# One bias table per distance, written as skewed DRAM rows, in a fused attention and token mixer

## The chip, the cores and the metric

The kernel runs on one core of one Trainium2 chip. The metric is the device time of one execution in microseconds (us). The kernel before has a median of 658.86 us over three runs (658.49 to 1035.87).

## The reference

Four batches of eight heads of attention over 576 positions with 64 columns a head, with a learned bias on the scores, and behind it a token mixer and a channel mixer over the 512 columns of a position:

```python
rel = (pos[:, None] - pos[None, :]).astype(np.float32)
psi_rel = np.log1p(np.abs(rel))
psi_i = np.log1p(np.maximum(pos[:, None].astype(np.float32), 1.0))
x = (psi_rel / psi_i)[..., None]
h = np.maximum(x @ w1 + b1, 0.0)          # 32 hidden values for each (i, j)
bias = h @ w2                             # 8 heads
scores = scores + bias.transpose(2, 0, 1)[None]
...                                       # softmax over j, times v
h = np.maximum(xt @ w_tok1, 0.0) @ w_tok2
u = x + h.transpose(0, 2, 1)
h2 = np.maximum(u @ w_ch1, 0.0) @ w_ch2
return u + h2
```

The bias depends on the query i and on the distance |i - j| alone, and is the same for all batches: 8 x 576 x 576 numbers. Since psi_i is positive, relu(w1 psi_rel / psi_i + b1) is relu(w1 psi_rel + b1 psi_i) / psi_i, and this is how the kernel computes it: rectify first, divide at the end.

## The kernel before

**The bias stage** (lines 457 to 488) works on 36 blocks of 16 queries. Partition p of a working tile holds one of 32 hidden units for one of four queries, so a block has four tiles of 128 x 576. `lw` holds w1 log1p(|distance|) over 1148 columns, each group of 32 partitions shifted by one column for its query; `rectify` (L440) cuts the window of 576 columns that belongs to the block and applies relu(window + b1 psi_i). Three of the four tiles are done on VectorE (DVE, L446), the fourth on ScalarE (ACT, L444), fixed. `mm` (L465, matmuls on L468) contracts the 32 hidden units with w2 into 8 heads: 8 fp32 matmuls of 288 columns, two halves for each of the four tiles, into the four quarters of one of two PSUM pairs, so that a pair holds 16 queries x 8 heads on its partitions. `over` (L471, on ACT at L474 or DVE at L476) multiplies by 8 / psi_i and writes one of 10 SBUF buffers (`eb`). `put` (L478) stores it to DRAM (`bd`) as 128 rows of 576 numbers, one contiguous 288 KB. 8 / psi_i itself is made by `inverse` (L451): a reciprocal and a product on DVE over 36 columns, a planned step that every `over` waits for.

Beside it, eight transfers of a padded copy of `v` (640 KB each) feed the 80 bf16 matmuls of L502, from whose diagonal a scale for `v` is taken.

**The attention** runs 16 units (two heads of one batch). Four times, for each pair of heads, `bias_load` (L644) reads the bias from DRAM: four transfers of 576 KB (128 queries x 2 heads, 4608 contiguous bytes a partition) and two small ones. For each 128 queries: scores (L717), bias and row maximum on DVE (L726), exp on ACT (L739), transposes on the tensor engine (L768) or, for two of five chunks, by DMA (L757), the products with `v` (L795 to L797). All bias matmuls come ahead of the first scores (`drawn`).

**The mixers**: the token mixer follows each unit; the channel mixer (L1017 to L1019, L1047 to L1049) has the last 300 us to itself.

**The order of the work** is not written by hand: each step is given costs per engine (`on`), a due time out of the table `DUE` (relative to a base of its block or unit), and what it follows, and `Plan.order` simulates the engines and emits the steps in the order found. A step with several engines (`over`) is given to the one that would end it first. Each engine, and SyncE and ACT as issuers of DMAs, then runs its instructions in that order, waiting where something is not there yet.

Of the kernel before, what the change touches and what calls it, by code (L numbers as in the profile page):

```python
# [8 lines left out]
F32 = mybir.dt.float32  # L9
# [14 lines left out]
TAB = 1148  # L24
# [11 lines left out]
SLACK = 0.129  # L36
STAY = 63.41
# [4 lines left out]
TURN = 1.5  # L42
# [11 lines left out]
ON = {'dlo': {'P': 1.9},  # L54
      'norm': {'V': (0.35, -36.79), 'A': (0.88, 3.18)},
      'over': {'A': 0.65, 'V': (0.72, 56.73)},
      'vh': {'P': (0.7, -16.17), 'V': (0.4, 23.01), 'A': (0.6, -13.17)},
      'vl': {'P': (1.36, 74.11)}}
DUE = {'blk': 46.13,
       'blkn': 2.08,  # L60
       'rect': -232.71,
       'bmm': -134.22,
       'over': -120.58,
       'put': -73.24,
       'bl': -42.04,
       'bln': 5.97,
       'sums': -151.84,
       'sumsn': 8.17,
       'measw': 90.24,
       'measwn': 4.78,  # L70
       'amax': 104.25,
       'scales': 323.07,
       'scalet': -281.84,
       'scalec': -178.66,
       'fill': -14.62,
       'fill1': 162.6,
       'tok': -57.19,
       'tokn': 3.24,
       'dec1': 79.36,
       'dec2': 61.91,  # L80
       'dec3': 106.38,
       'dec4': 116.76,
       'dec5': -136.21,
       'load_k': 105.83,
       'load_q': -18.77,
       'split_k': -79.64,
       'split_q': 4.13,
       'load_v': -169.03,
       'prep_v': 43.7,
       'prep_vh': -255.82,  # L90
       'prep_vl': 312.44,
       'scores': -150.45,
       'biased': 127.67,
       'exp': 18.59,
       'hi': -44.42,
       'lo': -62.4,
       'turn': -60.26,
       'flip': -86.15,
       'fliphi': -282.11,
       'flip2': 4.2,  # L100
       'fliplo': 90.47,
       'back': 106.94,
       'norm': -39.66,
       'mix0': -165.12,
       'mix1': 14.09,
       'relu': 5.56,
       'mix2': -169.29,
       'mix2b': -31.55,
       'store': 8.59,
       'w1': 54.35,  # L110
       'w1n': 17.85,
       'U0': 98.45,
       'U0n': -0.8,
       'U1n': -20.63,
       'U1': 4.3,
       'U2': 346.79,
       'Un': 3.06,
       'U3': 76.01,
       'U4': 222.06,
       'u1': 171.18,  # L120
       'u2': 58.41,
       'u3': 147.24,
       'u4': 38.89,
       'u5': 75.81,
       'G': 366.02,
       'G0': 89.88,
       'G0n': 7.58,
       'g1': 58.66,
       'g2': 70.33,
       'ur': 38.78,  # L130
       'w2m': -44.97,
       'w2mn': 7.09}
# [123 lines left out]
def attention_mixer(ctx, tc, qT, kT, v, cst, lg, ident, wt1, wt2, wc1, wc2, out, dump=None):  # L256
# [106 lines left out]
    with tc.manual_schedule():  # L363
# [45 lines left out]
        eb_t = [slots[:, 3 if i < 4 else 1, S * (i % 4 if i < 4 else i - 4):][:, 0:S] for i in range(EB_BUFS)]  # L409
        cs, lw, wf = (slots[:, 3, 4 * S + a:4 * S + b] for a, b in ((0, 190), (190, 190 + TAB), (190 + TAB, 222 + TAB)))  # L410
# [4 lines left out]
        bd = [ud.tile([128 if c < NCH else LEFT, NH * S], F32, name=f"bd{c}") for c in range(NCH + 1)]  # L415
# [35 lines left out]
        def inverse(e):  # L451
            V.reciprocal(out=ips, in_=ips)
            V.tensor_scalar(out=ips, in0=ips, scalar1=8.0, scalar2=None, op0=ALU.mult)

        ips_ok = add({"V": 0.4}, DUE["blk"] + DUE["over"], inverse)
        sums_all, mms = [], []
        for n, (c, o) in enumerate([(c, o) for c in range(NCH + 1) for o in range(8 if c < NCH else 4)]):
            q0 = 128 * c + 16 * o
            t = DUE["blk"] + DUE["blkn"] * n
            hs = Hold("rect")  # L460
            room = add({"-": 0.0}, t, lambda e: None, after=[room], take=[hs])
            rs = [add({"A": 0.68} if g == 3 else {"V": 0.47}, t + DUE["rect"], rectify(hs, g, q0 + 4 * g, 4 * n + g), after=[room], port=True) for g in range(4)]
# [18 lines left out]
            m = add({"T": 1.05}, t + DUE["bmm"], mm, after=rs, take=[ph], free=[hs], mode=3)  # L481
# [3 lines left out]
            bias_s.setdefault(c, []).append(add(wire("put", 1.0), t + DUE["put"], put, after=[v_], free=[eh]))  # L485
            bias_all.extend(bias_s[c][-1:])
            if n == 0:
                m2 = big.tile([128, 32], F32, name="m2")
                last, late = None, []
                vh_ = Hold("bank")  # L490
                for i in range(8):
                    h = Hold("sums")

                    def load(e, i=i, h=h):
                        ENG[e].dma_start(out=staging(h.i, 1280).rearrange("p (a x) -> p a x", a=2), in_=v[2 * i:2 * i + 2].rearrange("a p x -> p a x"))

                    def sums(e, i=i, h=h):

                        t = staging(h.i, 1280).bitcast(BF16).rearrange("p (n t) -> p n t", t=2)[:, :, 1]
                        for k in range(10):  # L500
                            x = t[:, k * 128:(k + 1) * 128]
                            PE.matmul(out=banks[vh_.i][:, 0:128], lhsT=x, rhs=x, start=(i == 0 and k == 0), stop=(i == 7 and k == 9))  # L502

                    x = add(wire("sums", 2.1), DUE["sums"] + DUE["sumsn"] * i, load, take=[h])
                    late.append((x, i))
                    last = add({"T": 0.68}, DUE["sums"] + DUE["sumsn"] * i + 6, sums, after=[x, last], take=[vh_] if i == 0 else [], free=[h], use=[vh_])
                    sums_all.append(last)
# [135 lines left out]

        def bias_load(hp, t0):  # L644
# [19 lines left out]
        def unit(u):  # L664
# [37 lines left out]
            for c in range(NCH + 1):  # L702
# [42 lines left out]
                if dma:  # L745
# [15 lines left out]
                    turned_s.append(add({"X": 1.8}, t + DUE["turn"], turn, after=[s], take=ta[:1], free=[p2]))  # L761
# [360 lines left out]
def lay_out(q, k, v, w1, b1, w2, moe_w_tok1, moe_w_tok2, moe_w_ch1, moe_w_ch2):  # L1122
    import numpy as np

    def heads(x):
# [17 lines left out]
    m = np.minimum(np.abs(np.arange(TAB)[None, :] - 572 - np.arange(4)[:, None]), S - 1)  # L1143
    lg = np.repeat(lrel[m], 32, axis=0)
# [6 lines left out]
        "qT": qq, "kT": kk, "v": vv,  # L1151
# [22 lines left out]
```

## Time and profile before

| | |
|---|---|
| median of the runs | 658.86 us |
| the profiled execution | 660.83 us |
| its span, first to last instruction | 659.0 us |
| PE (TensorE), busy | 624.8 us |
| DVE (VectorE), busy | 439.1 us |
| ACT (ScalarE), busy | 373.7 us |
| POOL (GpSimd), busy | 285.0 us |
| moved by DMA | 101.87 MB |
| mean granted TensorE clock | 0.984 of full |

The profiled execution is one run with the hardware profiler on; 1.8 us of it lie outside the span. Times in the rows below count from the start of the span. Busy time of the PE is from modelled ends of matmuls: a busy PE is not a PE at its peak.

### The profile page before, as it was taken

The page shows a single profiled execution, that of the slowest core. Times are in us where ns is not written, and L with a number is a line of the kernel's source. Part 1 is how long each engine was busy: PE and PEld are TensorE (multiplying, and loading weights), DVE is VectorE, ACT ScalarE, POOL GpSimd, SP SyncE. Part 2 cuts the span into 40 slices and gives each one's busy share as a digit, 9 for nine tenths or more (in the row PEclk, how much of TensorE's full clock was granted, in tenths as well). Part 3 has the DMA queues.
Part 4 walks back from the last instruction along what each step waited for, and adds up shares of the span by engine and source line. Part 5 has one row for each costly group of instructions (what it writes and reads, how often), then busy time and mean ns, then how long its engine had stood idle before and what let it go on. Part 6 is the DMA issues. An engine that isn't in the chain of part 4 may idle for free.

```text
span 659.0 us, 16970 instructions
## 1 busy us (share of the span) xinstructions
PE 624.8 (95%) x6820; PEld 421.6 (64%) x6820; DVE 439.1 (67%) x1125; ACT 373.7 (57%) x665; POOL 285.0 (43%) x328
## 2 busy tenths in 40 slices
PE   3988798799999999999999999999999999999996
PEld 1433587699898998988998864444444444465442
DVE  5799679988999899999999887877510220121000
ACT  5889668877887989888887644554311220021000
POOL 3020568795556878888743551665800000000000
PEclk9899789999999999999999999999999999999999
DMA  9997845699985945455544599656242001110211
GB/s 331 304 325 258 214 95 143 188 263 262 257 215 169 280 110 143 144 131 161 116 85 108 141 318 303 209 162 168 49 127 65 33 0 33 64 33 12 82 52 32
DMA packets 88511, 101.87 MB, mean 155 GB/s; under 512 B 49392, under 2 KB 58864, under 8 KB 88432
## 3 DMA queue, kind: packets, MB, share of 16 engines
q1 hardware_dynamic: 78784, 80.04, 43.7%
q10 hardware_dynamic: 9648, 20.75, 10.7%
q8 instruction: 53, 0.87, 0.6%
q14 instruction: 26, 0.21, 0.1%
HBM read 69.69 MB, written 20.05 MB: 136 GB/s over the span
## 4 chain that ended last, share of the span: by engine, by line
PE 73%; DVE 9%; DMA 7%; ACT 7%; POOL 2%; issue 2%; SPq 0%; ACTq 0%; DVEq 0%; POOLq 0%
PE pair L717 8%; PE bank L768 7%; PE bank L1048 7%; PE bank L1049 7%; PE bank L1047 7%; PE bank L1017 6%; PE bank L1018 6%; PE bank L1019 6%; PE pair L468 4%; DMA raw<-wc 4%; PE bank L795 2%; PE bank L797 2%; PE bank L796 2%; DVE t2a L774 2%; DVE z L726 2%
## 5 line engine op out<-in xcount | busy, mean ns | idle before, releaser
L739 ACT ACTIVATE z<-z,mx 128x576 f32<-128x576 f32 (+1 forms) x120 | 92.5, 779 | 15.6 <-DVE mx L726 14.2
L726 DVE CUSTOM_DVE_ANT_0 z<-pair,slots 128x576 f32<-128x576 f32 (+1 forms) x120 | 89.6, 756 | 6.1 <-PE pair L717 3.0
L1058 DVE SCALAR_TENSOR_TENSOR o<-bank,crow,ur 128x512 f32<-128x512 f32 x18 | 13.5, 751 | 112.5 <-PE bank L1049 112.5
L774 DVE SCALAR_TENSOR_TENSOR t2a<-bank,t2a 128x384 f16<-128x384 f32 (+1 forms) x150 | 79.8, 536 | 11.5 <-ACT t2a L771 10.0
L771 ACT ACTIVATE t2a<-bank 128x384 f16<-128x384 f32 (+1 forms) x150 | 70.3, 474 | 24.2 <-PE bank L768 18.9
L768 PE MATMUL bank<-id,z 128*128 128x128 f32 x469 | 76.9, 289 | 3.2 <-ACT z L739 2.0
L717 PE MATMUL pair<-kh,qh 64*128 64x288 f32 (+1 forms) x288 | 62.4, 352 | 6.8 <-DVE mx L726 6.3
L1017 PE MATMUL bank<-slots 128*128 128x384 f16 (+1 forms) x192 | 67.7, 353 | 0.3 <-DVE g1l L1027 0.3
L1018 PE MATMUL bank<-slots 128*128 128x384 f16 (+1 forms) x192 | 67.7, 352 | 0.0
L1019 PE MATMUL bank<-slots 128*128 128x384 f16 (+1 forms) x192 | 67.7, 352 | 0.0
L1039 ACT ACTIVATE ur<-ur,sc 128x512 f32<-128x512 f32 x18 | 13.0, 722 | 94.6 <-DMA ur<-um 81.1
L768 PEld LDWEIGHTS bank<-id,z 128*128 128x128 f32 x469 | 52.3, 145 | 12.4 <-issue 4.5
L795 PE MATMUL bank<-vh,t2a 128*128 128x65 f16 x558 | 59.7, 196 | 0.0
L796 PE MATMUL bank<-vl,t2a 128*128 128x64 f16 x558 | 59.5, 192 | 0.0
L797 PE MATMUL bank<-vh,t2a 128*128 128x65 f16 x558 | 59.4, 194 | 0.0
L717 PE MATMUL pair<-kl,qh 64*128 64x288 f32 (+1 forms) x288 | 52.8, 303 | 0.0
L796 PEld LDWEIGHTS <-t2a 128*128 128x128 f16 x558 | 51.8, 99 | 0.6
L795 PEld LDWEIGHTS <-t2a 128*128 128x128 f16 x558 | 51.6, 97 | 0.5 <-issue 0.2
L797 PEld LDWEIGHTS <-t2a 128*128 128x128 f16 x558 | 51.6, 97 | 0.0
L717 PE MATMUL pair<-kh,ql 64*128 64x288 f32 (+1 forms) x288 | 51.6, 297 | 0.0
L1047 PE MATMUL bank<-w2h,slots 128*128 128x512 f16 x132 | 50.0, 379 | 0.0
L1048 PE MATMUL bank<-w2l,slots 128*128 128x512 f16 x132 | 50.0, 379 | 0.0
(201 smaller groups left out, 1788.7 us busy)
## 6 DMA issues: line engine op xcount, KB each, us to landing
raw<-wc SPq DMA_DIRECT2D x48, 512.0 KB, 4.4
bd<-slots SPq DMA_DIRECT2D x36, 288.0 KB, 4.2
slots<-bd SPq DMA_DIRECT2D x16, 576.0 KB, 6.1
slots<-v SPq DMA_DIRECT2D x8, 640.0 KB, 6.3
tv<-v ACTq DMA_DIRECT2D x16, 320.0 KB, 3.4
qq<-qT ACTq DMA_DIRECT2D x16, 320.0 KB, 3.9
kk<-kT ACTq DMA_DIRECT2D x16, 320.0 KB, 4.1
um<-x SPq DMA_DIRECT2D x16, 256.0 KB, 3.3
```

The lines of the kernel that those rows point to most:

```text
L717: PE.matmul(out=pairs[both[h].i][:, 512 - i + n * i:512 + n * i], lhsT=qx[x][w, c * 128:c * 128 + 128], rhs=kx[y][w, k0:k0 + i], start=(j ...
L726: V.tensor_tensor_reduce(out=st["z"][z.i][:, o], in0=pairs[ph.i][:, 512 - i:512 + i], in1=bias_m[hp][:, c, h, :] if c < NCH else bias_l[hp ...
L768: PE.transpose(banks[tb.i][:, n * 128:(n + 1) * 128], st["z"][z.i][:, 384 * i + n * 128:384 * i + (n + 1) * 128], id32)
L774: V.scalar_tensor_tensor(out=block(h.i, 3, m), in0=banks[tb.i][:, 0:128 * m], scalar=P_SCALE, in1=block(h.i, 0, m), op0=ALU.mult, op1=ALU. ...
L795: PE.matmul(out=o, lhsT=lh, rhs=vh[:, n, 0:D + 1], start=(i == 0), stop=False)
L796: PE.matmul(out=ps[:, h, 0:D], lhsT=lh, rhs=vl[:, n, :], start=False, stop=False)
L797: PE.matmul(out=o, lhsT=ll, rhs=vh[:, n, 0:D + 1], start=False, stop=(i == 4))
L1017: PE.matmul(out=ps[:, 0:n], lhsT=w[0][:, c], rhs=uh[:, c], start=(c == 0), stop=False)
L1018: PE.matmul(out=ps[:, 0:n], lhsT=w[0][:, c], rhs=ul[:, c], start=False, stop=False)
L1019: PE.matmul(out=ps[:, 0:n], lhsT=w[1][:, c], rhs=uh[:, c], start=False, stop=(c == 3))
L1047: PE.matmul(out=ps, lhsT=gh_[:, f, w], rhs=wh[:, f], start=(f == 0), stop=False)
L1048: PE.matmul(out=ps, lhsT=gh_[:, f, w], rhs=wl[:, f], start=False, stop=False)
```

## The change

- `lw` shrinks to 576 columns, one per distance, the same on all partitions.
- `rectify` computes relu(lw + b1 psi_i) for the distances that the block needs, `far` = max(q0 + 16, 576 - q0) columns (576 at both ends, 304 in the middle), not for 576 keys. Each of the four tiles may now go to ACT or DVE, as the planner finds.
- `mm` reads those rows backwards (step -1) for the keys left of the query and forwards for the others: 591 output columns, 15 more than keys, in two pieces (28 blocks) or three (8 blocks), for each of four tiles. All 16 queries of a block share one base.
- `over` and `put` carry 591 columns; the DRAM rows have a pitch of 704 numbers, and each block is put at an offset so that all rows of a chunk share a common base.
- `bias_load` reads with a row step one number short of the pitch, which takes the skew back: two runs of 576 numbers a partition instead of one of 1152.
- The reciprocal of psi_i is made before the loop, not as a planned step.
- The `v` copy for the scale is unpadded: eight transfers of 576 KB, 72 matmuls instead of 80.
- The planner's costs (`turn` 1.8 to 1.1, `TURN` 1.5 to 0.0, and those of the edited steps), its `SLACK` and `STAY`, and nearly all due times are new; so the order of the whole kernel is.

```diff
-TAB = 1148
+SKEW = 15
+PITCH = 704
...
-SLACK = 0.129
-STAY = 63.41
+SLACK = 0.119
+STAY = 39.58
...
-TURN = 1.5
+TURN = 0.0
...
+EB = 592
...
+      'rect': {'A': (0.68, -0.04), 'V': 0.45},
...
-        A.dma_start(out=lw[:, 572:TAB], in_=lg[:, 572:TAB])
+        A.dma_start(out=lw[:, 0:288], in_=lg[:, 0:288])
         SP.dma_start(out=cs, in_=cst)
-        SP.dma_start(out=lw[:, 0:572], in_=lg[:, 0:572])
+        SP.dma_start(out=lw[:, 288:S], in_=lg[:, 288:S])
...
-        V.tensor_scalar(out=lw[:, 572:TAB], in0=lw[:, 572:TAB], scalar1=w1s, scalar2=None, op0=ALU.mult)
-        A.activation(out=lw[:, 0:572], in_=lw[:, 0:572], func=ACTF.Copy, scale=w1s)
-
-        def rectify(h, g, q, k):
+        V.reciprocal(out=ips, in_=ips)
+        V.tensor_scalar(out=ips, in0=ips, scalar1=8.0, scalar2=None, op0=ALU.mult)
+        V.tensor_scalar(out=lw[:, 0:288], in0=lw[:, 0:288], scalar1=w1s, scalar2=None, op0=ALU.mult)
+        A.activation(out=lw[:, 288:S], in_=lw[:, 288:S], func=ACTF.Copy, scale=w1s)
+
+        def rectify(h, g, n, k):
             def do(e):
-                r, win = rect_t[4 * h.i + g], lw[:, 572 - q:572 - q + S]
+                r, win = rect_t[4 * h.i + g][:, 0:n], lw[:, 0:n]
...
-        def inverse(e):
-            V.reciprocal(out=ips, in_=ips)
-            V.tensor_scalar(out=ips, in0=ips, scalar1=8.0, scalar2=None, op0=ALU.mult)
-
-        ips_ok = add({"V": 0.4}, DUE["blk"] + DUE["over"], inverse)
...
+            back_, ahead = q0 + SKEW, S - q0
+            far = max(back_ + 1, ahead)
...
-            rs = [add({"A": 0.68} if g == 3 else {"V": 0.47}, t + DUE["rect"], rectify(hs, g, q0 + 4 * g, 4 * n + g), after=[room], port=True) for g in range(4)]
+            rs = [add(share(ON["rect"], far / S), t + DUE["rect"], rectify(hs, g, far, 4 * n + g), after=[room], port=True) for g in range(4)]
             ph, eh = Hold("pair"), Hold("eb")
-
-            def mm(e, hs=hs, ph=ph):
-                for x in range(2):
+            zero = 512 if max(back_, ahead) <= 512 else 1024 - ahead if ahead > 512 else back_
+
+            def mm(e, hs=hs, ph=ph, zero=zero, a=zero - back_, b=zero + ahead):
+                ends = sorted({a, zero, 512, b})
+                for y0, y1 in zip(ends, ends[1:]):
                     for g in range(4):
-                        PE.matmul(out=pairs[ph.i][NF * g:NF * g + NF, 224 + 288 * x:512 + 288 * x], lhsT=wf.rearrange("p g h -> p (g h)"),
-                                  rhs=rect_t[4 * hs.i + g][:, 288 * x:288 * x + 288], start=True, stop=True)
-
-            def over(e, ph=ph, eh=eh, n=n):
-                x, y = pairs[ph.i][:, 224:800], eb_t[eh.i]
+                        r = rect_t[4 * hs.i + g]
+                        PE.matmul(out=pairs[ph.i][NF * g:NF * g + NF, y0:y1], lhsT=wf.rearrange("p g h -> p (g h)"),
+                                  rhs=r[:, y0 - zero:y1 - zero] if y0 >= zero else r[:, zero - y0:zero - y1:-1], start=True, stop=True)
+
+            def over(e, ph=ph, eh=eh, n=n, a=zero - back_, b=zero + ahead):
+                x, y = pairs[ph.i][:, a:b], eb_t[eh.i]
...
-                ENG[e].dma_start(out=bd[c][16 * o:16 * o + 16].rearrange("q (h j) -> (q h) j", j=S), in_=eb_t[eh.i])
+                a = 127 - SKEW - 16 * o
+                ENG[e].dma_start(out=bd[c][16 * o:16 * o + 16].rearrange("q (h j) -> (q h) j", j=PITCH)[:, a:a + S + SKEW], in_=eb_t[eh.i])
...
-            v_ = add(ON["over"], t + DUE["over"], over, after=[m, ips_ok], take=[eh], free=[ph])
+            v_ = add(ON["over"], t + DUE["over"], over, after=[m], take=[eh], free=[ph])
...
+        def rows_of(c, h, n):
+
+            x = bd[c][:, h * PITCH:(h + n) * PITCH]
+            return bass.AP(tensor=x.tensor, offset=x.offset + 127, ap=[[NH * PITCH - 1, x.shape[0]], [PITCH, n], [1, S]])
+
...
-                                      lambda e, c=c: ENG[e].dma_start(out=slots[:, hp % 2, c * PW:(c + 1) * PW], in_=bd[c][:, hp * PW:(hp + 1) * PW]), after=[*bias_s[c], *after])]
+                                      lambda e, c=c: ENG[e].dma_start(out=bias_m[hp][:, c], in_=rows_of(c, 2 * hp, 2)), after=[*bias_s[c], *after])]
...
-                    turned_s.append(add({"X": 1.8}, t + DUE["turn"], turn, after=[s], take=ta[:1], free=[p2]))
+                    turned_s.append(add({"X": 1.1}, t + DUE["turn"], turn, after=[s], take=ta[:1], free=[p2]))
```

## Rows read from the trace of the kernel before

**Rows 1.** The page: busy us of each engine, share of the span, instructions.
```profile
PE 624.8 (95%) x6820; PEld 421.6 (64%) x6820; DVE 439.1 (67%) x1125; ACT 373.7 (57%) x665; POOL 285.0 (43%) x328
```
**Rows 2.** Stretches (start:end length), busy of each engine, granted clock, DMA share, GB/s.
```profile
5.80:14.50 8.70, 4.60 (x32) 2.10 (x32) 7.89 (x19) 4.97 (x8) 3.10 (x8) 0.94 1.03 403
14.50:41.00 26.50, 25.20 (x332) 12.28 (x336) 20.90 (x47) 22.06 (x35) 2.44 (x2) 0.89 0.95 327
41.00:68.00 27.00, 21.82 (x304) 8.26 (x296) 24.24 (x53) 24.06 (x37) 5.24 (x5) 1.00 0.83 273
68.00:90.00 22.00, 17.10 (x123) 13.96 (x124) 15.29 (x41) 13.53 (x24) 14.89 (x33) 0.73 0.76 162
90.00:140.00 50.00, 43.82 (x702) 37.88 (x701) 44.48 (x129) 39.94 (x77) 39.85 (x50) 0.98 0.59 177
200.00:360.00 160.00, 158.98 (x2705) 144.87 (x2700) 151.45 (x418) 136.62 (x259) 113.24 (x117) 1.00 0.55 145
360.00:654.00 294.00, 293.61 (x1659) 147.36 (x1655) 117.31 (x263) 81.69 (x138) 67.43 (x68) 1.00 0.36 105
```
**Rows 3.** The chain of work that ended last, start us, us, what.
```profile
10.58 2.65 DVE slots L446 x6
13.22 0.30 DVE slots L452
13.55 0.20 DVE slots L453
14.56 2.15 PE pair L468 x16
```
**Rows 4.** The timeline, start us, us, engine, line, what, count, [idle before].
```profile
4.90 0.77 ACT L438 ACTIVATE slots<-slots 128x572 f32<-128x572 f32 x1 [2.24 <-DMA slots<-lg]
5.84 4.60 PE L468 MATMUL pair<-slots 128*32 128x288 f32 x32 [5.84 <-POOL slots L326]
...
17.82 2.15 PE L468 MATMUL pair<-rect,slots 128*32 128x288 f32 x16
```
**Rows 5.** The chain in the steady part of the bias stage.
```profile
53.19 0.78 ACT slots L444
53.97 0.64 ACT slots L474
54.65 1.30 PE pair L468 x16
```
**Rows 6.** Groups by line up to 68.6 us: shapes, count, busy us, mean ns, idle before.
```profile
L474 ACT ACTIVATE slots<-pair,slots 128x576 f32<-128x576 f32 x36 | 25.9, 726 | 3.6 <-DVE slots L453 2.4 <-PE pair L468 1.2
L444 ACT ACTIVATE slots<-slots 128x576 f32<-128x576 f32 x18 | 13.8, 770 | 2.9 <-PE pair L468 2.1
```
**Rows 7.** The page's groups by line, a narrower ACT copy out of PSUM.
```profile
L771 ACT ACTIVATE t2a<-bank 128x384 f16<-128x384 f32 (+1 forms) x150 | 70.3, 474 | 24.2 <-PE bank L768 18.9
```
**Rows 8.** The timeline where the PE is pushed: sums, then two blocks.
```profile
31.01 0.75 PE L502 MATMUL bank<-slots 128*128 128x128 bf16 x10
31.69 1.18 PE L468 MATMUL pair<-rect,slots 128*32 128x288 f32 x16
32.74 1.18 PE L468 MATMUL pair<-slots 128*32 128x288 f32 x16
```
**Rows 9.** The timeline where POOL works beside DVE's rectifying.
```profile
44.49 2.74 DVE L446 TENSOR_SCALAR rect<-slots 128x576 f32<-128x576 f32 x3 [0.17 <-PE pair L468]
44.61 1.80 POOL L339 TENSOR_TENSOR kl<-kk,kh 128x640 fp32r<-128x640 f32 x1 [24.04 <-PE pair L468]
```
**Rows 10.** A stretch in which the stores of the bias are nearly all of the DMA.
```profile
50.00:60.00 10.00, 8.39 (x116) 2.92 (x112) 10.00 (x24) 9.45 (x15) 0.00 (x0) 1.00 0.68 214
```
**Rows 11.** The chain behind the bias stage.
```profile
67.86 7.56 DMA qq<-qT
```
**Rows 12.** DMA issues: count, KB each, median us from issue to landing.
```profile
slots<-v SPq DMA_DIRECT2D x8, 640.0 KB, 6.3
rect<-rect SPq DMA_TRANSPOSE x32, 2.8
```

More of the change, by code (lines that the diff above doesn't have):

```diff
@@ L54 @@
 ON = {'dlo': {'P': 1.9},
[L55 to L81, printed above, removed]
-       'dec4': 116.76,
[L83 to L116, printed above, removed]
-       'Un': 3.06,
[L118 to L132, printed above, removed]
@@ new lines @@
+      'norm': {'V': (0.35, -30.99), 'A': (0.88, 27.47)},
+      'rect': {'A': (0.68, -0.04), 'V': 0.45},
+      'over': {'A': 0.66, 'V': (0.73, 80.22)},
+      'vh': {'P': (0.7, -17.04), 'V': (0.4, -20.86), 'A': (0.6, -38.5)},
+      'vl': {'P': (1.36, 115.17)}}
+DUE = {'blk': -9.3,
+       'blkn': 2.41,
+       'rect': -128.18,
+       'bmm': -151.76,
+       'over': -238.25,
+       'put': -213.24,
+       'bl': 9.61,
+       'bln': 7.08,
+       'sums': -192.54,
+       'sumsn': 6.75,
+       'measw': 56.82,
+       'measwn': 6.78,
+       'amax': 132.38,
+       'scales': 266.47,
+       'scalet': -341.65,
+       'scalec': -233.88,
+       'fill': -34.5,
+       'fill1': 166.33,
+       'tok': -104.82,
+       'tokn': 2.42,
+       'dec1': -2.23,
+       'dec2': 120.18,
+       'dec3': 197.17,
+       'dec4': 116.76,
+       'dec5': -134.92,
+       'load_k': 120.23,
+       'load_q': 15.55,
+       'split_k': -58.42,
+       'split_q': 116.64,
+       'load_v': -54.54,
+       'prep_v': 161.91,
+       'prep_vh': -156.03,
+       'prep_vl': 373.82,
+       'scores': -163.4,
+       'biased': 86.82,
+       'exp': 34.84,
+       'hi': 17.05,
+       'lo': -173.74,
+       'turn': -59.49,
+       'flip': -159.08,
+       'fliphi': -298.08,
+       'flip2': 2.2,
+       'fliplo': 10.9,
+       'back': 115.46,
+       'norm': -80.53,
+       'mix0': -245.87,
+       'mix1': 49.66,
+       'relu': -61.67,
+       'mix2': -209.52,
+       'mix2b': -56.06,
+       'store': 58.31,
+       'w1': 29.36,
+       'w1n': 19.85,
+       'U0': -37.07,
+       'U0n': -0.63,
+       'U1n': -19.27,
+       'U1': 36.69,
+       'U2': 255.56,
+       'Un': 3.06,
+       'U3': 71.03,
+       'U4': 207.83,
+       'u1': 178.13,
+       'u2': -21.71,
+       'u3': 126.96,
+       'u4': 111.51,
+       'u5': 95.89,
+       'G': 295.33,
+       'G0': 133.43,
+       'G0n': 9.58,
+       'g1': 68.49,
+       'g2': -52.89,
+       'ur': 14.23,
+       'w2m': -167.36,
+       'w2mn': 8.27}
@@ L255, in attention_mixer @@
 @with_exitstack
-def attention_mixer(ctx, tc, qT, kT, v, cst, lg, ident, wt1, wt2, wc1, wc2, out, dump=None):
+def attention_mixer(ctx, tc, qT, kT, v, vt, cst, lg, ident, wt1, wt2, wc1, wc2, out, dump=None):
     nc = tc.nc
@@ L408, in attention_mixer @@
         rect_t += [more[:, S * i:S * i + S] for i in range(8)]
-        eb_t = [slots[:, 3 if i < 4 else 1, S * (i % 4 if i < 4 else i - 4):][:, 0:S] for i in range(EB_BUFS)]
-        cs, lw, wf = (slots[:, 3, 4 * S + a:4 * S + b] for a, b in ((0, 190), (190, 190 + TAB), (190 + TAB, 222 + TAB)))
+        eb_t = [slots[:, 3 if i < 4 else 1, EB * (i % 4 if i < 4 else i - 4):][:, 0:S + SKEW] for i in range(EB_BUFS)]
+        cs, lw, wf = (slots[:, 3, 4 * EB + a:4 * EB + b] for a, b in ((0, 190), (190, 190 + S), (190 + S, 222 + S)))
         wf = wf.rearrange("p (g h) -> p g h", g=4)
@@ L494, in load @@
                     def load(e, i=i, h=h):
-                        ENG[e].dma_start(out=staging(h.i, 1280).rearrange("p (a x) -> p a x", a=2), in_=v[2 * i:2 * i + 2].rearrange("a p x -> p a x"))
+                        ENG[e].dma_start(out=slots[:, 0, 1152 * h.i:1152 * h.i + 1152], in_=vt[i])
                     def sums(e, i=i, h=h):
-                        t = staging(h.i, 1280).bitcast(BF16).rearrange("p (n t) -> p n t", t=2)[:, :, 1]
-                        for k in range(10):
+                        t = slots[:, 0, 1152 * h.i:1152 * h.i + 1152].bitcast(BF16).rearrange("p (n t) -> p n t", t=2)[:, :, 1]
+                        for k in range(9):
                             x = t[:, k * 128:(k + 1) * 128]
-                            PE.matmul(out=banks[vh_.i][:, 0:128], lhsT=x, rhs=x, start=(i == 0 and k == 0), stop=(i == 7 and k == 9))
-                    x = add(wire("sums", 2.1), DUE["sums"] + DUE["sumsn"] * i, load, take=[h])
+                            PE.matmul(out=banks[vh_.i][:, 0:128], lhsT=x, rhs=x, start=(i == 0 and k == 0), stop=(i == 7 and k == 8))
+                    x = add(wire("sums", 1.9), DUE["sums"] + DUE["sumsn"] * i, load, take=[h])
                     late.append((x, i))
-                    last = add({"T": 0.68}, DUE["sums"] + DUE["sumsn"] * i + 6, sums, after=[x, last], take=[vh_] if i == 0 else [], free=[h], use=[vh_])
+                    last = add({"T": 0.61}, DUE["sums"] + DUE["sumsn"] * i + 6, sums, after=[x, last], take=[vh_] if i == 0 else [], free=[h], use=[vh_])
                     sums_all.append(last)
```

15 lines of the change are left out of this document (6 added, 9 removed).

## The prediction

> **What bounds the kernel now.** The busy totals come first [rows 1]: PE 625 of 659 us, the others far below. That is an average, so the stretches come next [rows 2]. From 360 us on the PE is busy 293.6 of 294 us, and from 200 to 360 us 159.0 of 160 with DVE at 151: there the PE sets the pace, and of this change only the order of the work and the loads of the bias reach it. What can be won lies ahead of that, where the PE is not full: in the bias stage, which ends at 67.9 us [rows 11], and in the run-up of the attention, 68 to 140 us.
>
> [...] First a stall: the PE has done two blocks by 10.4 us and stands still until 14.56 [rows 3, 4], because both PSUM pairs are full and `over` waits for the reciprocal of psi_i, which DVE reaches only after eighteen rectifying steps; from 5.8 to 14.5 us the PE is busy 4.60 of 8.70 us. [...] Third, the steady pace: the chain goes ACT rectify (0.78), ACT `over` (0.64), PE, and round again [rows 5], so a block takes 1.42 us, set by ACT, with DVE nearly as full (24.2 of 27 us and 10.0 of 10 [rows 2, 10]). The PE alone needs less: 1.05 from block to block where it is pushed, and 0.68 for ten sums [rows 8].
>
> **The change, part by part.** The sum is made against the profiled execution, 660.8 us (span 659.0, 1.8 outside), which is 2.0 above the median of the runs.
>
> *Start.* The reciprocal and its product (0.30 + 0.20 [rows 3]) now stand ahead of DVE's first rectifying, and the first block needs both halves of `lw`. ACT's scaling starts at 4.90, when its half lands, and halves from 0.77 to 0.4 [rows 4], so rectifying starts near 5.4 instead of 5.0; the first matmul waited for POOL until 5.84 anyway [rows 4]. Cost 0.3.
>
> *The stall* goes: 8.70 - 4.60 = 4.1 won. What comes late next is the rectifying itself. *The lower clock* goes with it, since nothing else idles the PE before 20 us: 2 x (2.15 - 1.18) = 1.9 won.
>
> *The pace.* A block needs on average 440 of 576 columns rectified, mean of max(q0 + 16, 576 - q0). Six DVE steps take 2.65, so 0.44 each [rows 3]; a DVE step of 36 columns takes 0.20 there, so the part that doesn't shrink lies between 0 and about 0.18, and the step of 440 columns between 0.34 and 0.38: I take 0.36. On ACT, 576 columns cost 0.77 as rectifying and 0.73 as `over` [rows 6], 384 columns 0.47 [rows 7]; that makes 0.58 for 440, and 0.655 for `over` in the chain's measure, 0.64 x 591/576 [rows 5]. With `over` on ACT and x of the four tiles too, 0.66 + 0.58 x = 0.36 (4 - x) gives x = 0.83 and 1.14 us a block. The PE streams 591 columns, 1.05 x 591/576 = 1.08, and eight sums of nine, 8 x 0.61 / 36 = 0.14 a block: 1.22. So the PE, not ACT, would set the mean pace; blocks at both ends are wide (DVE and ACT need 1.34 there), buffers smooth that only in part, and 8 blocks have four short matmuls more. I take 1.25. Thirty-four blocks follow the stall: 34 x (1.42 - 1.25) = 5.8 won. From 14.56 to 67.9 the old stage took 53.3 us; less 1.9 for the clock and 48.3 for 34 blocks leaves 3.1 for episodes such as the one at 44.5 us, where three DVE steps take 2.74 beside POOL's subtraction [rows 9]. Those remain.
>
> *Reading backwards.* No row shows a product with a reversed operand. Nearest are the forward ones [rows 8]: at best the same, at worst several times that for the reversed half. I take the same, because an fp32 product already spends 1.05 us on 2304 columns, four tiles at a time.
>
> *The transfers.* In 50 to 60 us the DMA moves 214 GB/s, nearly all stores of the bias, at a share of 0.68 [rows 10], so full it would carry 315, and a store of 295 KB costs 0.94. Now each is 303 KB in 128 runs of 2364 bytes at a pitch; each bias load has 256 runs instead of 128. Below, this costs nothing; above, the dearest rate nearby is that of 68 to 90 us, 162 GB/s at 0.76, full 213 [rows 2], which makes a store 1.42. I take the bytes alone, 0.96, because the runs are as long as the old stores' rows. From 5.8 to 68 us the DMA worked 57 us (share times length of the stretches [rows 2]). Unpadded sums save 0.5 of 5.2 MB [rows 12], 1.3 us, the longer stores add 0.7: 56, for which some 50 are left. Ten buffers let the PE run ahead of the stores by ten blocks, 9.4 us, so the PE doesn't wait; the last stores end some 6 us behind it.
> [...]
>
> *Elsewhere.* The units keep every instruction. The planner's time for a DMA transpose falls; the trace has 2.8 us from issue to landing [rows 12]. If the new figure is too short, PE steps are placed a little early, hidden while other products stand ahead of them. [...] The order of 68 to 140 us is new and can't be read from the diff: old holes there may close, new ones open. I put 1.0 as the part of the gain that late stores and loads take back.
>
> Sum: -0.3 + 4.1 + 1.9 + 5.8 - 1.0 = 10.5 off. 660.8 - 10.5 = 650.3 profiled, **648** by the median.
>
> **The rivals.**
> *A, the run-up shrinks too.* From 68 to 140 us the PE idles 22.0 - 17.1 + 50.0 - 43.8 = 11.1 us, and its 17.1 busy us at a clock of 0.73 [rows 2] would be 12.5 at full clock, 4.6 less. The first hole is a late load of q, 7.56 us [rows 11]. With DVE and ACT freed, decoding of weights may move into the bias stage, where POOL is nearly idle (5.2 of 27). Against it: DVE is at 44.5 of 50 in 90 to 140, and its work isn't less. Half of the 15.7 gives 640.
> *B, the transfers or the new order take it back.* DMA share is 0.95 and 1.03 in the early stretches [rows 2]. If a store costs half way to the upper bound, 1.18, the work from 5.8 us on grows by 36 x 0.22 to 64 us; the PE may end 9.4 before it, at 60, and the last rows land near 70. Half the gain is gone: 655.
> *C, slower: reversed reads.* The place is the left piece of each product, mean 295 of 591 columns, 0.54 us. At r times the price, the stage ends at 5.9 + 4.9 (sums) + 36 (0.54 + 0.54 r) = 30 + 19.4 r. Below r = 1.35 the pace above decides; at 1.95 nothing is won; at 2 the stage ends at 69, all scores wait for it, and the time is 660; at 4 it ends at 108 and the time is 699. Against it: each of the four tiles streams a column in 1.8 ns (1.05 us for 576), where a bf16 sum takes 0.53 (0.68 us for 1280) [rows 8], so the reading has room.
> *D, the change does less than it says:* ACT keeps one rectifying of each block and the rows of the chain stay; then the pace is 0.58 + 0.66 = 1.24 and the sum is the forecast's.
>
> **How the numbers follow.** Forecast with D (644 to 653): 0.44. A: 0.27. B: 0.21. C: 0.08. The range leaves out what lies under 636, where the run-up would have to give 12 of its 15.7, and over 661, C from r = 2 up: 636 to 661; the forecast's own is 644 to 653. The bound of 2%, about what a measurement of this kernel can tell from no change, is 645.7 and 672.0. Faster by more: A and the low edge of the forecast, 0.27 + 0.08 = 0.35. Slower by more: C from r = 2.6, where the stage ends 13.2 us later than before, 0.05. Within: 0.60.
>
> **What would show it.** Right: first `over` near 6.5 us, no PE hole before 20 us, a granted clock near 1.0 over 14.5 to 41, blocks at 1.1 to 1.35 us, with DVE taking about three tiles of a wide block and more of a narrow one, last bias matmul at 54 to 58. Wrong by C: a matmul on reversed rows longer than a forward one of its width. Wrong by B: stores over 6 us to landing and `over` waiting for a buffer. By A: an idle PE of under 6 us in the 72 us behind the stage. The prediction fails if the stage ends as forecast and the stretch up to the steady attention grows by more than 5 us.

## The result, and the profile after

The changed kernel takes **650.34 us** (median of four runs, 647.18 to 652.28); the kernel before, run beside it on the same chip, 659.21. The ratio is 0.987 [0.983, 0.990], so the change saves 8.9 us. One of the four runs of the kernel before took 1035.87 us; without it its median is 658.86 and the saving 8.5. The profiled execution took 647.18 us, its span 645.3; the profiled one of the kernel before took 660.83.

The busy row of the page, which answers to [rows 1]:
```profile
PE 619.5 (96%) x6876; PEld 417.9 (65%) x6876; DVE 432.8 (67%) x1130; ACT 374.7 (58%) x676; POOL 273.4 (42%) x312
```
The PE has 5 us less to do and its idle time has gone from 34.2 to 25.8 us: most of the gain is idle time lost.

The stretches of [rows 2], read from the changed kernel (start:end length, busy us of PE, PEld, DVE, ACT and POOL, granted clock, DMA share, GB/s):
```profile
5.80:14.50 8.70, 8.56 (x140) 3.94 (x144) 8.70 (x23) 6.94 (x12) 0.00 (x0) 1.00 1.02 392
14.50:41.00 26.50, 23.48 (x330) 10.99 (x326) 21.38 (x61) 20.89 (x37) 10.70 (x14) 0.94 0.93 324
41.00:68.00 27.00, 23.91 (x307) 12.95 (x299) 22.47 (x60) 22.54 (x36) 9.02 (x26) 0.87 1.02 362
68.00:90.00 22.00, 18.27 (x253) 15.57 (x253) 19.65 (x54) 17.84 (x34) 15.47 (x18) 0.92 0.47 125
90.00:140.00 50.00, 47.47 (x773) 42.16 (x773) 46.51 (x132) 41.98 (x80) 39.85 (x47) 1.00 0.80 235
200.00:360.00 160.00, 159.25 (x2697) 144.47 (x2698) 149.91 (x415) 138.09 (x261) 101.57 (x103) 1.00 0.56 138
20.00:25.00 5.00, 5.00 (x60) 2.26 (x64) 2.82 (x9) 3.77 (x7) 2.71 (x10) 0.73 0.69 237
```
The first line shows the stall gone: the PE is busy 8.56 of 8.70 us where it was busy 4.60. The second and third show that this is not a stage without holes: the PE is busy 23.5 of 26.5 us, so it idles 3.0 us where it idled 1.3, and the last line shows the granted clock down at 0.73 in 20 to 25. The DMA share in 41 to 68, 0.83 before, is 1.02. From 200 to 360 us nothing has changed: the PE is still full.

The timeline of the changed kernel around these places (start us, us, engine, line, what, [idle before]); L447 is DVE's rectifying, L475 `over` on ACT, L469 the bias products, L327 the first step of the split of `k`:
```profile
4.72 2.64 DVE L447 TENSOR_SCALAR slots<-slots 128x576 f32<-128x576 f32 x6
5.39 4.37 PE L469 MATMUL pair<-slots 128*32 128x15 f32 x48 [5.39 <-DVE slots L447]
8.47 0.75 ACT L475 ACTIVATE slots<-pair,slots 128x591 f32<-128x591 f32 x1 [1.07 <-PE pair L469]
14.70 5.12 POOL L591 TENSOR_SCALAR dm<-raw 128x512 f32<-128x512 f32 x1 [10.03 <-DMA raw<-wt]
18.54 0.74 ACT L327 ACTIVATE kh<-kk 128x640 fp32r<-128x640 f32 x1 [2.17 <-DMA kk<-kT]
19.18 0.73 ACT L475 ACTIVATE slots<-pair,slots 128x591 f32<-128x591 f32 x1
19.97 3.50 PE L469 MATMUL pair<-slots 128*32 128x143 f32 x32 [2.34 <-ACT slots L475]
```
Rectifying starts at 4.72, the products at 5.39, the first `over` at 8.47 where it stood behind the stall before. A smaller hole is new: at 16.4 us ACT stops for a transfer of `k`, an `over` stands behind that step, and the PE idles 2.34 us until 19.97.

The bias products by line (the blocks whose rectified rows lie in the tile `rect` have this row, the others, whose rows lie in `slots`, a second one that ends sooner; count, least/median/most ns of one and first to last start). First the kernel before, whose last product starts at 67.3 us, then the changed one, at 56.5:
```profile
L468 PE MATMUL pair<-rect,slots x288: 406/406/690, 14.6 to 67.3; 128*32 128x288 f32 x144
L469 PE MATMUL pair<-rect,slots x320: 181/392/617, 9.5 to 56.5; 128*32 128x512 f32 x16, 128*32 128x47 f32 x8, 128*32 128x32 f32 x8, 128*32 128x63 f32 x8
```
The groups that answer to [rows 6], up to 57 us (shapes, count, busy us, mean ns, idle before):
```profile
L475 ACT ACTIVATE slots<-pair,slots 128x591 f32<-128x591 f32 x36 | 26.8, 748 | 4.7 <-PE pair L469 3.2 <-ACT rect L445 0.9
L445 ACT ACTIVATE rect<-slots 128x528 f32<-128x528 f32 (+13 forms) x16 | 10.3, 666 | 0.1
L445 ACT ACTIVATE slots<-slots 128x320 f32<-128x320 f32 (+13 forms) x15 | 9.6, 644 | 1.3 <-PE pair L469 1.2
```
ACT does 31 rectifyings where it did 36, and narrower ones; the other 113 of 144 are DVE's.

The chain behind the stage, which answers to [rows 11] (start us, us, what):
```profile
56.84 6.51 DMA qq<-qT
63.37 0.74 ACT qh L327
```
It has the same shape, a load of `q` of 6.51 us where there were 7.56, 11 us earlier.

From these traces the execution can be cut at three places: the start of the last bias product, the start of the last product of the last scores, and the end.

| profiled execution | last bias product | from there to the last scores | last scores to the end of the run | time |
|---|---|---|---|---|
| before | 67.3 | 293.4 | 300.1 | 660.83 |
| changed | 56.5 | 291.3 | 299.4 | 647.18 |
| changed, once more | 56.8 | 294.6 | 299.4 | 650.80 |

The stage gives 10.5 to 10.8 us. The run-up and the attention differ by 3.3 us between two executions of the changed kernel, 2.1 below and 1.2 above the one trace of the kernel before. The rest stays within 0.7 us. So what is to be explained is the stage, and how much of its gain is taken back.

### The profile page after: what moved, and what is told of

Its sections match the earlier page's. It is cut to its first block, busy times and chain, and to the rows that moved or that the text cites. A ratio compares the mean times of both kernels' runs of the same rounds, so it can differ in the third digit from the quotient of the medians.

```text
span 645.3 us, 17107 instructions
## 1 busy us (share of the span) xinstructions
PE 619.5 (96%) x6876; PEld 417.9 (65%) x6876; DVE 432.8 (67%) x1130; ACT 374.7 (58%) x676; POOL 273.4 (42%) x312
## 3 DMA queue, kind: packets, MB, share of 16 engines
q10 hardware_dynamic: 9648, 20.60, 10.6%
## 4 chain that ended last, share of the span: by engine, by line
PE 75%; DVE 11%; DMA 9%; ACT 3%; issue 1%; POOL 1%; ACTq 0%; DVEq 0%; SPq 0%
PE pair L724 8%; PE bank L775 8%; PE bank L1056 7%; PE bank L1054 7%; PE bank L1055 7%; PE bank L1024 6%; PE bank L1025 6%; PE bank L1026 6%; PE pair L469 4%; DMA raw<-wc 4%; PE bank L802 3%; PE bank L804 3%; PE bank L803 3%; DVE z L733 2%; DVE t2a L781 2%
## 5 line engine op out<-in xcount | busy, mean ns | idle before, releaser
L775 PE MATMUL bank<-id,z 128*128 128x128 f32 x469 | 75.5, 284 | 1.3 <-DVE t2a L781 0.7
L775 PEld LDWEIGHTS bank<-id,z 128*128 128x128 f32 x469 | 51.0, 142 | 10.1 <-issue 4.9
L597 POOL TENSOR_TENSOR dm<-dc,ds 128x512 f32<-128x512 f32 x24 | 30.8, 1284 | 45.8 <-DVE dc L594 29.9
```

The lines of the kernel that those rows point to most:

```text
L775: PE.transpose(banks[tb.i][:, n * 128:(n + 1) * 128], st["z"][z.i][:, 384 * i + n * 128:384 * i + (n + 1) * 128], id32)
```

## The experiments

Each ran beside the kernel before on the same chip; ratios are to that one.

**The changed kernel once more, the yardstick of the edits.**

> The changed kernel once more, unedited, as the yardstick for the runs beside it. Theory (a gain of the bias stage, kept to the end): 647 to 652 us, median near 650, last bias matmul starting at 56 to 58 us. If the 647.2 us of the profiled execution was the exception and the run-up loses more in most executions, the median lies at 651 or above.

Measured: 650.8 us, 0.987 [0.985, 0.990].

### The terms of the sum

**E1, the stall alone.** In the kernel before, the reciprocal stands ahead of the loop; the order is otherwise its own.
```diff
+        V.reciprocal(out=ips, in_=ips)
+        V.tensor_scalar(out=ips, in0=ips, scalar1=8.0, scalar2=None, op0=ALU.mult)
...
         def inverse(e):
-            V.reciprocal(out=ips, in_=ips)
-            V.tensor_scalar(out=ips, in0=ips, scalar1=8.0, scalar2=None, op0=ALU.mult)
+            pass
```


> The kernel before with one edit: the reciprocal of psi_i and its product are made ahead of the loop; the order of all else is the old one. Theory (stall and lower clock were worth 6.0 us of the bias stage): last bias matmul at about 61.5 us instead of 67.3, time 652 to 654. Rival (behind the stall the transfers or the old run-up decide, so what is saved early is waited for later): stage ends at 62 but the time is 656 or more.

Measured: 658.85 us, 1.000 [0.998, 1.002]. The stage ends at 69.5. The timeline of E1 says what came late next (L592 decodes the first token weight, the last line is a block's products):
```profile
17.50 0.67 ACT L592 ACTIVATE ds<-raw 128x512 f16<-128x512 f32 x1 [4.59 <-DMA raw<-wt]
19.52 1.90 PE L469 MATMUL pair<-slots 128*32 128x288 f32 x16 [4.22 <-ACT slots L475]
```
and its chain where that transfer begins:
```profile
4.31 13.17 DMA raw<-wt
```
ACT now reaches the decoding of a weight 4.59 us before the weight is there. Its 512 KB were issued at 4.31 and took 13.17 us, in a DMA whose share is 1.02 in 5.8 to 14.5. The `over` behind it waits, the pairs stay full, and the PE has a hole of 4.22 us in place of the old one of 4.1. In the kernel before, this weight landed at 14.8 us, as the stall ended, and only POOL and, for 1.04 us, DVE waited for it; for ACT and the PE the stall had hidden it:
```profile
14.82 0.89 POOL L589 TENSOR_SCALAR dm<-raw 128x512 f32<-128x512 f32 x1 [5.77 <-DMA raw<-wt]
```
In E1 the first stores of the bias are issued at 12.31 instead of 14.53, into the full DMA, and the weight lands 2.7 us later. That the stores push it back fits, and was not tried by itself.

**E10, that wait too.** E1, with the first token weight loaded ahead of `v`.
```diff
+        load_words("D", st["raw"][0], tok[0][0], 512)
```


> The kernel before with the reciprocal ahead of the loop and, in addition, the first token weight (512 KB) loaded ahead of the four transfers of v; order of all else unchanged. With the reciprocal alone ACT waited until 17.5 us for that weight, with over and the PE behind it for 4.2 us. Theory (the first stall only hid the wait for this transfer, and both must go): no PE hole of over 2 us before 20 us, last bias matmul at 62 to 64 us, time 653 to 656. Rival (what is saved early is lost to the next transfer or in the run-up): a new wait of 3 us or more before 45 us, or stage earlier and time still 657 to 659.

Measured: 659.43 us, 1.001 [0.999, 1.004]; the stage ends at 68.4. The timeline of E10 (L324 splits the first `k`):
```profile
19.05 0.74 ACT L324 ACTIVATE kh<-kk 128x640 fp32r<-128x640 f32 x1 [4.05 <-DMA kk<-kT]
20.36 0.72 ACT L476 ACTIVATE slots<-pair,slots 128x576 f32<-128x576 f32 x1
21.13 1.19 PE L470 MATMUL pair<-slots 128*32 128x288 f32 x8 [4.21 <-ACT slots L476]
```
A third wait of the same size: ACT for `k`, 4.05 us, and the PE behind it 4.21 us. In E1 that transfer was hidden behind the wait for the weight: ACT came to the same step at 19.38. Two waits removed one after the other gave nothing, the stage even ends 1.1 to 2.2 us later: each had the next one under it, and the last two are for transfers out of the same full DMA (a share of 1.02 in 5.8 to 14.5 us in both runs).

**E9, the stall put back into the changed kernel.** The reciprocal and its product are emitted ahead of the nineteenth rectifying step of DVE. The planned order puts some `over` steps ahead of that, so the first blocks are scaled by psi_i that is not yet inverted; the amount of work is the same.
```diff
-        V.reciprocal(out=ips, in_=ips)
...
+                    if len(count) == 19:
+                        V.reciprocal(out=ips, in_=ips)
```


> The changed kernel with the reciprocal of psi_i and its product put back behind eighteen of DVE's rectifying steps, order otherwise unchanged. [...] Rival (DVE and ACT work ahead in the stall and the later blocks catch up, or the transfers set the end of the stage): stage at most 2 us later, 650 to 652.

Measured: 649.28 us, 0.986 [0.983, 0.990]; the stage ends at 57.2. This says nothing on the stall, because those first `over` steps were in the order ahead of the reciprocal and waited for nothing. It shows only that the place of 0.5 us of DVE work is worth nothing.

**E3, the new tables with the old code.** The kernel before with the changed kernel's due times, costs, `SLACK`, `STAY` and turn costs: every block rectifies 4 x 576 columns, three tiles on DVE and one on ACT.
```diff
-SLACK = 0.129
+SLACK = 0.119
...                                     # DUE, ON, STAY, TURN likewise
```


> The kernel before planned with the new due times, SLACK, STAY, TURN and cost of a DMA transpose; its bias stage as it was. Theory (the edits make the gain): 657 to 664 us, bias stage ending at 62 us or later. Rival (the new plan makes it): 653 or less, with the run-up from the end of the stage to 140 us shorter than before.

Measured: 656.9 us, 0.998 [0.996, 1.001]. The bias products of E3 (columns as above):
```profile
L468 PE MATMUL pair<-rect,slots x288: 405/406/537, 9.8 to 56.9; 128*32 128x288 f32 x144
```
The old code ends the stage at 56.9, as early as the new one, while ACT does one rectifying and one `over` for every block. So the old rectifying was never what held the stage above 57. The stretches of E3 up to there:
```profile
5.80:14.50 8.70, 8.70 (x94) 4.23 (x98) 8.69 (x21) 7.93 (x12) 0.00 (x0) 1.00 1.02 387
14.50:41.00 26.50, 24.44 (x367) 12.29 (x363) 24.74 (x58) 25.16 (x39) 10.62 (x9) 1.00 1.01 360
41.00:57.00 16.00, 14.64 (x208) 5.21 (x200) 15.25 (x38) 15.86 (x25) 1.43 (x1) 1.00 0.87 319
```
The PE idles 3.4 us of these 51.2, at a granted clock of 1.00. In the kernel before it idles 10.6 us up to 68, at 0.94 and 0.89 in the first two stretches [rows 2]. The waits of E1 and E10 are out of the way all at once: the reciprocal runs at 4.60, ACT decodes its first weight at 25.31 and splits its first `k` at 54.70. And from 39.38 to 54.91 us the same instructions do twelve blocks at 1.29 us each where [rows 5] has 1.42, so that pace too was in part a matter of order. What E3 loses comes after. Its stretches behind the stage:
```profile
57.00:68.00 11.00, 7.69 (x52) 5.67 (x44) 6.66 (x17) 3.99 (x6) 8.16 (x13) 0.69 0.91 319
68.00:90.00 22.00, 16.19 (x157) 13.32 (x156) 17.12 (x39) 16.74 (x31) 15.59 (x31) 0.77 0.44 114
```
and its chain there:
```profile
57.52 4.71 DMA kk<-kT
62.31 6.01 DMA qq<-qT
68.35 0.74 ACT qh L324
```
Here `k` and then `q` are waited for, and `qh` starts at 68.35 where the changed kernel has it at 63.37. The PE works at a granted clock of 0.69 up to 68, as it does in the changed kernel, and of 0.77 in 68 to 90, against 0.92 there. From the last bias product to the last scores E3 takes 299.9 us against 293.4 before: 6.5 of the 10.4 us are given back. By the medians it is more: 1.1 us of time are left of them.

**E2, the new code with the old tables.**
```diff
-SLACK = 0.119
+SLACK = 0.129
...                                     # DUE, ON, STAY, TURN likewise; 'rect' stays
```


> The changed kernel planned with the old due times, SLACK, STAY, TURN and cost of a DMA transpose (rectifying still free to go to ACT or DVE). Theory (the edits of the bias stage make the gain, the new plan little): 649 to 654 us. Rival (the new plan makes it, or the old tables don't fit the new stage): 657 or more, with the stage still ending before 60 us and the loss in 60 to 140 us.

Measured: 673.7 us, 1.023 [1.020, 1.027]. The bias products of E2, and the first line of its channel mixer:
```profile
L469 PE MATMUL pair<-rect,slots x320: 181/392/1062, 12.2 to 67.4; 128*32 128x512 f32 x15, 128*32 128x47 f32 x9, 128*32 128x32 f32 x8, 128*32 128x63 f32 x8
L1024 PE MATMUL bank<-slots x192: 326/353/632, 370.4 to 612.8; 128*128 128x384 f16 x96, 128*128 128x512 f16 x96
```
The stage ends at 67.4, where the old one ended, though the reciprocal and the narrow rectifying are those of the changed kernel: in the old order the new code gains nothing there. The last product of the last scores starts at 357.6, 3.1 us sooner than before; but the channel mixer, which elsewhere begins some 5.5 us ahead of it, begins 12.8 us behind it, at 370.4. So the loss lies at the far end of the kernel, in steps that the edit does not touch; neither expectation had it there. What holds the channel mixer back was not tried.

**E5, full width.** The changed kernel rectifies 576 columns of every tile.
```diff
-... rectify(hs, g, far, 4 * n + g) ...
+... rectify(hs, g, S, 4 * n + g) ...
```


> The changed kernel with all 576 columns rectified in every block (the surplus is never read), order unchanged. Theory (the narrower rectifying is what quickened the pace): DVE's steps go back to 0.44 us and ACT's to 0.70 everywhere, a block takes about 1.35 instead of 1.15, the stage ends 5 to 7 us later and the time is 655 to 657. Rival (the DMA, at a share of 1.02 from 35 us on, or the PE sets the pace and hides the rectifying): stage at most 2 us later, 650 to 652.

Measured: 654.3 us, 0.993 [0.991, 0.996]; the stage ends at 60.4:
```profile
L469 PE MATMUL pair<-rect,slots x320: 181/394/995, 9.9 to 60.4; 128*32 128x512 f32 x15, 128*32 128x47 f32 x9, 128*32 128x32 f32 x8, 128*32 128x63 f32 x8
```
In this order the narrow rectifying is worth 3.6 us of stage and 3.5 us of time, under the 5 to 7 expected. DVE's 113 steps are busy for 54.2 us in E5 and for 44.0 in the changed kernel; of these 10 us about a third shows in the time.

**E4, the left piece read forwards.**
```diff
-... r[:, zero - y0:zero - y1:-1], ...
+... r[:, 0:y1 - y0], ...
```


> The changed kernel with the left piece of each bias product read forwards instead of backwards, widths and order unchanged; the left keys get the bias of wrong distances. Theory (reading backwards costs nothing): time within 1 us of the changed kernel run beside it, about 650, last bias matmul at 56 to 57 us, left and right pieces of equal width equally long. Rival (reversed reads cost, so part of the gain was lost there): the PE's bias matmuls get shorter by 10% or more, the stage ends 1 to 4 us earlier and the time is 646 to 649.

Measured: 651.83 us, 0.988 [0.985, 0.991]; no gain. The stage ends later than expected, at 58.8, because ACT's wait for `k` was longer in this execution (3.4 us against 2.17): the PE stands 3.6 us where it stood 2.34, and the granted clock behind it is 0.50 instead of 0.73:
```profile
20.00:25.00 5.00, 3.71 (x32) 1.57 (x36) 1.50 (x5) 3.78 (x6) 1.76 (x3) 0.50 0.44 170
```
Ends of the stage are therefore good to 1 or 2 us only. The shape-by-shape groups of the changed kernel (busy us, mean ns of one):
```profile
L469 PE MATMUL pair<-rect,slots 128*32 128x303 f32 x8 | 0.7, 430 | 0.0
L469 PE MATMUL pair<-slots 128*32 128x304 f32 x8 | 0.7, 419 | 0.0
```
303 columns are a reversed piece, 304 a forward one. In E4 these means are again 430 and 419, though the 303 are now read forwards. Reversal costs nothing that can be seen here; the 11 ns belong to the piece.

### The transfers

**E6, rows that start on a boundary.** Stores of 576 numbers at a multiple of 256 bytes, loads without the skew.
```diff
-... [:, a:a + S + SKEW], in_=eb_t[eh.i])
+... [:, 64:64 + S], in_=eb_t[eh.i][:, 0:S])
...
-... offset=x.offset + 127, ap=[[NH * PITCH - 1, ...
+... offset=x.offset + 64, ap=[[NH * PITCH, ...
```


> The changed kernel with stores and loads of the bias cut to 576 columns that start on a 256-byte boundary in DRAM, without the skew (so the keys get a shifted bias); order unchanged. Theory (the runs cost their bytes alone): DMA share over 41 to 68 us within 0.02 of the 1.02 of the changed kernel, stores about 6 us to landing, time 650 to 651. [...]

Measured: 651.32 us, 0.989 [0.986, 0.993]. The stretch of 41 to 68 us in E6, and its issues of the stores in 14.5 to 68 us (count, KB, median us to landing):
```profile
41.00:68.00 27.00, 22.68 (x305) 11.47 (x300) 20.91 (x58) 21.59 (x34) 6.93 (x10) 0.94 0.97 351
```
```profile
bd<-slots SPq DMA_DIRECT2D x32, 288.0 KB, 5.3
```
In the changed kernel a store takes 6.1 us to landing (6.5 in its second trace) and the share is 1.02. So a store lands 0.8 us sooner, with 2.5% fewer bytes in it, and the time does not move. The run doesn't part the boundary from the bytes.

**E7, half of the bytes.** Stores of 304 numbers a row, and loads that read as many bytes as before, in shorter runs.
```diff
-... [:, a:a + S + SKEW], in_=eb_t[eh.i])
+... [:, a:a + 304], in_=eb_t[eh.i][:, 0:304])
```


> The changed kernel storing 304 of the 591 columns of each bias row and reading the first half four times over (as many bytes read as before, the bias is wrong); order unchanged, some 5.3 MB less written in the first 65 us. Theory (the transfers, at a share of 1.02 from 35 to 65 us, hold up the end of the stage and the loads behind it): share falls to about 0.75, the load of q behind the stage lands in 4 us instead of 6.5, the k that ACT waits for in 16 to 19 us comes 2 us sooner, time 645 to 648. Rival (DVE sets the run-up, the transfers are hidden): the same loads come sooner but the time stays at 649 to 651.

Measured: 648.31 us, 0.985 [0.981, 0.989]. Its stretches and, behind the stage, its issues:
```profile
14.50:41.00 26.50, 24.49 (x363) 11.34 (x360) 24.34 (x64) 22.61 (x39) 8.82 (x15) 1.00 0.83 263
41.00:68.00 27.00, 22.65 (x283) 12.23 (x279) 22.53 (x62) 22.88 (x38) 8.06 (x25) 0.87 0.88 252
```
```profile
bd<-slots SPq DMA_DIRECT2D x32, 152.0 KB, 3.8
qq<-qT ACTq DMA_DIRECT2D x2, 320.0 KB, 3.6
```
The 3.6 us are the median of two loads of `q`, which is 5.2 in the changed kernel; the one behind the stage lands in 4.1 us instead of 6.51, and the stage ends at 55.1. Yet the time is only 2.0 to 2.5 us less, with overlapping intervals: halving the stores is worth that at most.

### The wait that is new

**E8, the first unit's `k` and `q` loaded at the start.**
```diff
+        A.dma_start(out=st["kk"][0], in_=kT[order_of[0]])
+        A.dma_start(out=st["qq"][0], in_=qT[order_of[0]])
```


> The changed kernel with the first unit's k and q loaded at about 2.7 us, ahead of the loop, instead of at 10.9 and 11.2; order otherwise unchanged. In the changed kernel ACT waits 2.2 us for that k at 16.4 us with over queued behind it, the PE stands 2.3 us and the clock falls to a mean of 0.73 in 20 to 25 us. Theory (that wait is the new stall of the stage): the wait goes, stage ends 3 us earlier, time 646 to 648 where the changed kernel has 650. Rival (the transfers, at a share of 1.0, only change places and the last stores decide the run-up): stage earlier by up to 3 us but the time within 1 us of the changed kernel.

Measured: 648.5 us (645.74 to 650.21), 0.985 [0.982, 0.988]. The stretches of E8:
```profile
14.50:41.00 26.50, 25.74 (x380) 12.94 (x383) 25.57 (x68) 23.62 (x41) 9.24 (x14) 1.00 0.99 340
20.00:25.00 5.00, 4.95 (x78) 2.51 (x71) 5.00 (x13) 4.77 (x9) 1.34 (x3) 1.00 0.91 287
```
The hole before 20 us is gone and the granted clock stays at 1.00, so the drop to 0.73 belonged to the hole, as the deeper one of E4 did to its longer hole. The stage ends at 54.9, with the PE busy 25.74 of 26.5. Of the 1.6 to 1.9 us of stage about as much reaches the medians, but the interval overlaps the changed kernel's. This is the best version found; that it beats the changed kernel is likely, not shown.

**E11, `q` of the second unit too.** E8, with that load right behind the second unit's `k`. The load comes ahead of a step that still reads the first unit's `q`, so the low half of the first unit's `q` is taken from the second's; the work is the same, and it is no version to use.
```diff
+                    if (u, tiles) == (1, "kk"):
+                        ENG[e].dma_start(out=st["qq"][0], in_=qT[order_of[1]])
```


> The changed kernel with the first unit's k and q loaded ahead of the loop (as in the run with the first loads), and with the second unit's q loaded right behind its k, at 39 us, instead of at 56.8 behind the stage; order otherwise unchanged. Theory (the chain behind the stage begins with that load, 6.5 us, and ACT's wait for it): no DMA of q in the chain between 55 and 65 us, run-up 1 to 3 us shorter, time 645 to 647. Rival (DVE is the bound of the run-up and the load is hidden): 648 to 649, as with the first loads alone.

Measured: 646.39 us (644.63 to 648.5), 0.982 [0.979, 0.986]. The wait for `q` is gone from the chain, and from the last bias product to the last scores it takes 291.5 us against E8's 296.3. But E8's trace is of its slowest run and E11's of its fastest, and one trace of the changed kernel has 291.3 with the wait in it. The medians differ by 2.1 us and the intervals overlap: some 2 us at most, as E7 says in its own way.

## Why the prediction was right, and where its steps were not

The forecast was 648, the stage end "at 54 to 58" and a give-back of 1.0. Measured: 650.3 and 56.5. The give-back is 1.2 by one trace of the changed kernel, while the other gains 2.1 (294.6 and 291.3 against 293.4). By the medians it is 1.9 and 2.8: 8.9 and 7.7 us of time are left of 10.8 and 10.5 of stage. The one trace of the kernel before is 1.6 us above its median, so the size of the give-back is not settled. The sum of the stage, 11.5 forecast, was right, and no run speaks for a rival: A would have shortened the run-up by 8 us, B would have left the stage near 60 and rows landing at 70, while the loads that read the last rows are issued from 64.17 on, when these have landed. ACT kept 0.86 of a tile a block, where the working had 0.83 and D one. In the 72 us behind the stage the PE idles 8.5 us, above the 6 set for A. Two terms of the sum were wrong all the same, in ways that cancelled: that the sum came out is luck.

**Stall and clock, 4.1 + 1.9.** The 1.9 is two blocks at 2.15 us [rows 3, 4] against 1.18 [rows 8]. The trace of the kernel before shows the clock that goes with them, 0.50 over 14.5 to 20 us and 1.00 over 20 to 68 (length, busy us of PE and PEld with the bias products alone, granted clock, DMA share, GB/s):
```profile
14.50:20.00 5.50, 4.33 (x36) 1.59 (x40) 0.50 1.03 343
20.00:68.00 48.00, 36.65 (x512) 13.49 (x504) 1.00 0.88 295
```
No run shows the 4.1 or the 1.9 as time won. The step said that the rectifying itself comes late next. E1 shows that at the place of the stall another wait of 4.2 us comes next, and E10 a third. Alone, in the old order, this step is worth nothing (1.000 and 1.001). I priced a hole as if what lies under it were ready. The row that warned stood in [rows 2]: a DMA share of 1.03 and 0.95 in just this stretch. In the changed kernel what remains of it is the wait for `k`, 2.34 us of PE, and a granted clock of 0.73 behind it, so "nothing else idles the PE before 20 us" fell too; E8 is the kernel that this step described.

**The pace, 5.8.** The new pace was sized well: from 27.2 to 54.1 us the changed kernel does 22 blocks at 1.22 us, 27 sums among them, where I took 1.25; DVE took 3.1 of four tiles. But E3 ends the stage at 56.9 with the old rectifying, and E5 puts the narrow one at 3.5 us in the new order. The error is in the old side of the difference. 1.42 was the steady pace of the old order, and the same code does 1.29 in E3's; and 36 blocks of 1.42 fill only 51 of the stage's 62 us. The other 10.4 were holes and time at the lower clock, of which I had counted 6.0, and put 3.1 aside as episodes that "remain".

So the 10.8 us of the stage are a matter of order first: the new tables with the old code give 10.4, the new code with the old tables none. The new code's part is what keeps them, since with the old code and the new tables 6.5 us are given back behind the stage. With the new code and the old tables 15.7 us of time are lost, at the far end. The 8.9 us of the change are not the sum of a part of the code (+15.7 by E2) and a part of the plan (-1.1 by E3, not separated from none). Why the same tables bring `q` 5 us later with the old code was not tried.

**Start.** 0.3 lost was forecast; rectifying began at 4.72 instead of 5.0, 0.3 won, as the constants landed at 3.54 instead of 4.20. The first `over` stood at 8.47, not near 6.5: the products of the first two blocks, which are wide, run as one stretch of 4.37 us from 5.39, and I had counted the rectifying alone.

**Reading backwards** at the same price: shown by E4. **The transfers** were denser than forecast: 6.1 us to landing and a share of 1.02, where B's mark was 6. But no `over` waited for a buffer, and E6 and E7 put what this costs at 0 to 2.5 us. **Elsewhere** nothing moved: from the first to the last product of the channel mixer every kernel takes 297.0 to 299.5 us, E2 too, so what is won or lost lies ahead of it.

## What to carry to other kernels

Before a stall is priced, ask what the same instruction stream waits for just behind it: here, at a DMA share of 1.02 to 1.03, holes of 4.1, 4.22 and 4.21 us lay one under the other, and taking one wait away showed only the next. Count a stage as blocks times pace plus holes, and check the old kernel by that sum first; here 51 of 62 us would have told that the holes, not the pace, were the larger part. Where a planner's tables order a kernel, code and tables are one change: run each with the other's partner before giving either the credit.

## What the runs showed of the hardware that was not expected

- A POOL product of 128 x 512 beside DVE's rectifying took 5.12 us in the changed kernel (14.70, above), while the two such products of E4 up to 60 us, in the same order, took 0.78 on average. It took 7.94 us in E3 (15.15), and 0.89 in the kernel before (14.82), where DVE idled for more than half of that time. In E1 it took 0.88 (17.55), and there three of DVE's steps begun at 17.84 were busy 1.76 us, where three begun at 25.36 took 1.37. So the same order can come out either way; no run shows what it cost.
- Loads of one size landed at different times: 512 KB issued at 4.31 us took 13.17 us in E1, with a DMA share of 1.02 in 5.8 to 14.5 and 0.81 in 14.5 to 20, where the 48 loads of 512 KB that the changed kernel issues from 90 to 436 us have a median of 4.6. 320 KB of `q` took 6.51 us behind the stage in the changed kernel, at a share of 1.01 meanwhile, and 4.1 in E7, where the stores were halved.
